# Inner matmul groups of two-level gate/up products wait for the token block they read

## The chip, the core and the metric

The kernel runs on one NeuronCore of a Trainium2 chip. The metric is device time in microseconds (us) for one execution. The engines are named as in the profile: PE is the tensor engine, PEld its weight loads, DVE the vector engine, ACT the scalar engine, POOL GpSimd and SP the engine that issues all DMAs here.

## What is computed

The input is one sequence of 2048 tokens of width 1024. Two kinds of layer alternate, A B A B, each with a residual and a layernorm ahead of it. Layer A is linear attention with 32 heads. Layer B is a bilinear gated block, and it is the one the change touches:

```
g = jnp.einsum("bsd,df->bsf", x, w_gate)      # d = 1024, f = 3584
u = jnp.einsum("bsd,df->bsf", x, w_up)
h = g * u
return jnp.einsum("bsf,fd->bsd", h, w_down)

x = x + _A_ref(_layernorm(x), A_wqkv, A_wo)
x = x + _B_ref(_layernorm(x), B_w_gate, B_w_up, B_w_down)
x = x + _A_ref(_layernorm(x), A_wqkv, A_wo)   # same weights again
x = x + _B_ref(_layernorm(x), B_w_gate, B_w_up, B_w_down)
```

## The kernel before

**Strassen products.** Layer B works on 1024 tokens at a time, so each of the two B layers has two passes (pass 0 and pass 1). Within a pass, a gate or up product of 256 feature columns by 1024 tokens is cut into 2 x 2 blocks and made from seven products instead of eight, named "1" to "7" (Strassen's method in Winograd's form). One such product is four matmuls of 512 columns, recorded at L1593. Some products, "1" and "5" in the first B layer and "1", "5", "3", "2" in the second, are cut a second time: seven inner products of two matmuls of 256 columns, recorded at L1663. The helper `l2_of` (L1634 on) sets these up. An inner group's left side is a block of weights or a sum of such blocks. Its right side is one of the four token blocks `b11`, `b12`, `b21`, `b22` of the operand, or one of three sums of them (`tp[0]` to `tp[2]`). Steps named `st1` (inner products 1 and 5), `st6`, `st7` and `direct` (inner products 2, 3, 4) issue them.

**One block is overwritten.** Inner product 7 needs `b22 - b12`, and the kernel writes that in place of `b12`. In the first pass of the first B layer, the first pair of gate/up units still uses "1" and "5" in their plain form and so needs `b12` unchanged. There the overwriting DVE operation is held back (the table `XD`) and is issued between the first pair and the second: for "1" after the elementwise product that the order table calls M5A, for "5" after M5B. The later passes overwrite `b12` ahead of time, among the layernorm work.

**What sets the order and the waits.** All work is put down by `P.add(engine, function, rd=..., wr=...)` in one fixed sequence; a string table `ORDERS` gives the sequence within a pair of units. Each engine runs its own list strictly in order. What an operation waits for comes from its ranges of bytes: `rd` and `wr` are looked up by pages of 32 bytes, and the operation depends on the last writer of every page it reads. `plan` then drops a wait that an earlier wait on the same engine already covers, and `emit` puts the first remaining wait on the operation's first instruction and each further wait ahead of it as an instruction of its own. A wait holds everything behind it on that engine.

Before the change, the four token blocks share one list of ranges `rx`, that of the whole operand, so an inner group that reads `b11` also depends on the last writer of `b12`.

The other names in the profile: L841 is the helper `tt` of all DVE additions, subtractions and multiplications in SBUF, L844 the helper `stt`, L1682 the DVE addition `join` that puts a sum of inner products into a PSUM bank, L1679 and L1689 the two ACT copies behind `st1`, L1598, L1607, L1773 and L1623 other ACT copies out of PSUM, L1499 the last product of layer A and L2104 and L2012 the down products.

Of the kernel before, what the change touches and what calls it, by code (L numbers as in the profile page):

```python
# [176 lines left out]
def _seg(base, n, stride, lo, hi):  # L177
    return [(base + i * stride + lo, base + i * stride + hi) for i in range(n)]


def build_kernel(nc, A_x, A_wqkv, A_wo, B_w_gate, B_w_up, B_w_down, out):
    _, S, D = A_x.shape
# [40 lines left out]
    def take(n, align=64):  # L223
        nonlocal off
        off = (off + align - 1) // align * align
        o = off
        off += n
        return o

    O_X = take(NST * D * 2)  # L230
    O_XT = take(KT * S * 2)
# [22 lines left out]
    O_T = RB  # L254
# [79 lines left out]
    with ExitStack() as es:  # L334
# [13 lines left out]
        def vh(o, n):  # L348
            return ah[:, o // 2: o // 2 + n]
# [72 lines left out]
        def R(o, n):  # L422
            return [(o, o + n)]
# [1133 lines left out]
        def layer_B(lnp, nxt, first):  # L1557
# [3 lines left out]
            def pair(ps_, p, l2):  # L1561
                s0 = ps_ * 1024
# [81 lines left out]
                def l2_of(q):  # L1644
# [9 lines left out]
                    wB, rB = units[1]["w"][q]  # L1654
                    x, rx = xb[q]
                    tp = [(vh(o, 512).rearrange("p (k s) -> p k s", s=256), R(o, 1024)) for o in (O_TP0 if jit else O_TP)[q]]
                    b11, b12, b21, b22 = [(x[:, 2 * k:2 * k + 2, 256 * c:256 * c + 256], rx) for k in range(2) for c in range(2)]
                    qs = {1: ((wA[:, 0:2, :], rA), b11), 2: ((wA[:, 2:4, :], rA), b21), 3: ((sp[3], rp[3]), b22), 4: ((wB[:, 2:4, :], rB), tp[2]),
                          5: ((sp[0], rp[0]), tp[0]), 6: ((sp[1], rp[1]), tp[1]), 7: ((sp[2], rp[2]), b12)}

# [68 lines left out]
                    return dict(st1=st1, st6=st6, st7=st7, st5=add5, direct=direct, s=s_of)  # L1729

                L = {q: l2_of(q) for q in l2}

                def fold_cp():
# [606 lines left out]
```

## Time and profile before

| | us |
|---|---|
| median of 3 runs | 1441.0 (1439.71 to 1441.69) |
| profiled execution | 1437.69 |
| its span, first to last instruction | 1436.0 |
| PE busy in it | 1423.3 (99%) |
| DVE busy | 1166.5 (81%) |
| ACT busy | 733.3 (51%) |
| mean DMA rate | 230 GB/s |

The granted clock of PE was 1.000 over the span. Times below are counted from the span's start. The first B layer's pass 0 begins about 238 us and its down products at 408 us; the second B layer's two passes begin about 955 us and 1192 us. A busy PE is the sum of pipelined matmul records, each of which lasts longer than the distance to the next one, so an idle time of PE as shown is a little shorter than the time by which the next matmul comes late.

### The profile page before, as it was taken

The numbers are of one execution on the slowest core, as the hardware profiler recorded it, in microseconds if no ns is written. First come the engines' busy times: TensorE is split into PE (matmuls) and PEld (weight loads), VectorE is DVE, ScalarE is ACT, GpSimd is POOL, SyncE is SP. The second block draws the span as 40 slices with busy tenths as digits, with TensorE's granted clock in tenths as the row PEclk, the third lists the DMA queues.
The fourth block names the chain that finished last, engine by engine and source line by source line (L and its number), as shares of the span: only waits on it lengthen the run. The fifth ranks groups of instructions, "written<-read, shape, count | busy, mean of one in ns | idle before, by whom it ended". The sixth has DMA issues, their size and how long they took to land.

```text
span 1436.0 us, 22438 instructions
## 1 busy us (share of the span) xinstructions
PE 1423.3 (99%) x8388; PEld 809.3 (56%) x8388; DVE 1166.5 (81%) x2012; ACT 733.3 (51%) x1538; POOL 314.2 (22%) x321
## 2 busy tenths in 40 slices
PE   9999999999999999999999999999999999999999
PEld 4444444555544455554764444456666477666658
DVE  7878887889879789878778878779877867777886
ACT  4752367677731155552256523567777115777521
POOL 4643632000013000003334346300000400000060
PEclk9999999999999999999999999999999999999999
DMA  6316868887878899995898067679985699778668
GB/s 234 107 26 189 178 137 199 244 292 243 298 262 286 283 320 315 274 271 177 261 362 207 34 188 154 151 216 270 280 271 198 227 284 324 256 258 265 211 185 258
DMA packets 393996, 330.15 MB, mean 230 GB/s; under 512 B 178336, under 2 KB 342048, under 8 KB 393376
## 3 DMA queue, kind: packets, MB, share of 16 engines
q1 hardware_dynamic: 393888, 328.72, 76.3%
q8 instruction: 66, 1.08, 0.3%
q14 instruction: 42, 0.34, 0.1%
HBM read 238.49 MB, written 66.58 MB: 212 GB/s over the span
## 4 chain that ended last, share of the span: by engine, by line
PE 95%; DVE 2%; ACT 1%; DMA 1%; issue 1%; SPq 0%; POOL 0%; DVEq 0%
PE ps L1593 27%; PE ps L1663 18%; PE ps L2104 14%; PE ps L2012 8%; PE ps L1401 8%; PE ps L1499 6%; PE ps L1167 6%; PE ps L971 5%; PE ps L981 3%; DVE arena L841 1%; PE ps L1413 1%; PE ps L1441 0%; DMA arena<-in_A_x_dram 0%; DVE arena L481 0%; SPq L441 0%
## 5 line engine op out<-in xcount | busy, mean ns | idle before, releaser
L841 DVE TENSOR_TENSOR arena<-arena 128x512 f16<-128x512 f16 (+9 forms) x780 | 480.6, 644 | 76.7 <-ACT arena L1707 45.1
L1593 PE MATMUL ps<-arena 128*128 128x512 f16 x1808 | 446.9, 379 | 0.6 <-ACT ps L1623 0.6
L1663 PE MATMUL ps<-arena 128*128 128x256 f16 x2324 | 312.2, 273 | 6.0 <-DVE arena L841 5.3
L844 DVE SCALAR_TENSOR_TENSOR arena<-ps,arena 128x512 f16<-128x512 f32 (+2 forms) x392 | 259.8, 684 | 38.8 <-PE ps L1593 16.3
L1663 PEld LDWEIGHTS ps<-arena 128*128 128x128 f16 (+1 forms) x2324 | 226.1, 98 | 109.8 <-DVE arena L841 6.3
L1593 PEld LDWEIGHTS ps<-arena 128*128 128x128 f16 (+1 forms) x1808 | 176.5, 98 | 141.7 <-ACT ps L1623 1.1
L2057 POOL TENSOR_TENSOR arena<-arena 128x512 f32<-128x512 f32 x56 | 87.3, 1564 | 596.5 <-ACT arena L2055 591.4
L2104 PE MATMUL ps<-arena 128*128 128x512 f16 (+1 forms) x952 | 206.9, 379 | 0.0
L1598 ACT ACTIVATE arena<-ps 128x512 f16<-128x512 f32 x224 | 133.9, 598 | 92.9 <-PE ps L1593 90.8
L2104 PEld LDWEIGHTS ps<-arena 128*128 128x128 f16 x952 | 93.1, 98 | 111.5
L1682 DVE TENSOR_TENSOR ps<-ps,arena 128x256 f32<-128x256 f32 x220 | 92.3, 428 | 39.5 <-PE ps L1663 23.0
L1679 ACT COPY ps<-ps 128x256 f32<-128x256 f32 x220 | 81.1, 369 | 84.3 <-PE ps L1663 78.0
L2012 PE MATMUL ps<-arena 128*128 128x256 f16 (+1 forms) x1078 | 119.1, 273 | 0.2
L1401 PE MATMUL ps<-arena 128*128 128x512 bf16 x512 | 115.4, 379 | 0.0
L2012 PEld LDWEIGHTS ps<-arena 128*128 128x128 f16 x1078 | 104.8, 98 | 14.2 <-DVE ps L2019 0.4
L1499 PE MATMUL ps<-arena 128*128 128x512 bf16 x512 | 111.5, 379 | 0.0
L2055 ACT ACTIVATE arena<-ps 128x512 f32<-128x512 f32 x48 | 28.7, 597 | 132.6 <-PE ps L2104 132.6
L1167 PE MATMUL ps<-arena 128*128 128x512 bf16 (+1 forms) x420 | 95.1, 379 | 0.4 <-DVE ps L1171 0.3
L1307 POOL TENSOR_TENSOR arena<-arena 128x1024 f16<-128x1024 f32 x32 | 80.0, 2501 | 69.1 <-DVE arena L1305 62.7
L1623 ACT COPY ps<-ps 128x512 f32<-128x512 f32 x112 | 64.2, 573 | 50.3 <-PE ps L1663 45.0
L1006 POOL TENSOR_TENSOR arena<-arena 128x512 f32<-128x512 f32 x60 | 73.5, 1244 | 69.4 <-DVE arena L1096 33.7
L1499 PEld LDWEIGHTS ps<-arena 128*128 128x128 f16 x512 | 50.1, 98 | 59.8
(80 smaller groups left out, 1261.6 us busy)
## 6 DMA issues: line engine op xcount, KB each, us to landing
arena<-w_scratch SPq DMA_DIRECT2D x84, 512.0 KB, 5.7
arena<-sp_scratch SPq DMA_DIRECT2D x56, 512.0 KB, 5.8
arena<-t_scratch SPq DMA_DIRECT2D x27, 896.0 KB, 5.6
arena<-in_B_w_down_dram SPq DMA_DIRECT2D x18, 896.0 KB, 6.7
w_scratch<-arena SPq DMA_DIRECT2D x28, 512.0 KB, 6.4
sp_scratch<-arena SPq DMA_DIRECT2D x28, 512.0 KB, 4.8
arena<-in_B_w_gate_dram SPq DMA_DIRECT2D x42, 256.0 KB, 5.3
arena<-in_B_w_up_dram SPq DMA_DIRECT2D x42, 256.0 KB, 3.2
```

The costliest lines, as they stand in the source:

```text
L841: P.add("dve", lambda e: e.tensor_tensor(out=out, in0=a, in1=b, op=op), rd=rd, wr=wr, prd=prd)
L844: P.add("dve", lambda e: e.scalar_tensor_tensor(out=out, in0=a, scalar=sc, in1=b, op0=ALU.mult, op1=op1), rd=rd, wr=wr, prd=prd)
L1167: P.add("pe", lambda e: [e.matmul(psb(bank), x[:, k, :], w[:, k, :], start=(start and k == 0), stop=(k == 3), skip_group_check=True) for k ...
L1401: return [e.matmul(psb(bank), xr[:, t, j * 128:(j + 1) * 128], pk[:, h, t, :], start=(t == 0), stop=(t == NST - 1)) for t in range(NST)]
L1499: return [e.matmul(psb(bank), xnT[:, g, i * 128:(i + 1) * 128], wp[:, g, dh * 512:(dh + 1) * 512], start=(dh == 0 and g == 0), stop=(g == ...
L1593: P.add("pe", lambda e: [e.matmul(psb(bank), w[:, k, :], x[:, k, :], start=(start and k == 0), stop=(k == 3), skip_group_check=True) for k ...
L1598: P.add("act", lambda e: e.activation(t, psb(bank), AF.Copy, scale=SG), prd=[bank], wr=r)
L1663: P.add("pe", lambda e: [e.matmul(psb(bank)[:, 256 * half:256 * half + 256], w[:, k, :], xx[:, k, :], start=(start and k == 0), stop=(k == ...
L1682: P.add("dve", lambda e: e.tensor_tensor(out=psb(dst[c])[:, 256:512], in0=lo, in1=c5, op=ALU.add), prd=[bk], rd=rc5, pwr=[dst[c]])
L2012: P.add("pe", lambda e: [e.matmul(psb(bank)[:, 256 * half:256 * half + 256], a[:, k, :], w[:, k, :], start=(start and k == 0), stop=(k == ...
L2057: P.add("pool", (lambda k2, x: lambda e: e.tensor_tensor(out=rtmp[k2], in0=rtmp[k], in1=x, op=ALU.add))(k2, x), rd=rx + rr(k), wr=rr(k2))
L2104: return [e.matmul(psb(bank), hv[:, 7 * hf + k, t * 128:(t + 1) * 128], w[:, k, :], start=(start and hf == 0 and k == 0), stop=(hf == 1 an ...
```

## The change

The whole-operand range is replaced by the range of the block that is read. For "5" in the form of the temporary T1 the rows are 1024 bytes apart, for "1", "2" and "3" they are rows of the transposed activations. No instruction is added, removed or moved on any engine; what waits for what is different. The lines behind it move down by five, so that L1663 becomes L1668.

```diff
-                    b11, b12, b21, b22 = [(x[:, 2 * k:2 * k + 2, 256 * c:256 * c + 256], rx) for k in range(2) for c in range(2)]
+                    if q == "5":
+                        base, st_ = O_T, 1024
+                    else:
+                        base, st_ = O_XT + 4 * (q != "1") * S * 2 + 2 * s0 + 1024 * (q == "3"), S * 2
+                    b11, b12, b21, b22 = [(x[:, 2 * k:2 * k + 2, 256 * c:256 * c + 256], _seg(base + 2 * k * st_, 2, st_, 512 * c, 512 * c + 512))
+                                          for k in range(2) for c in range(2)]
```

PE, first B layer, pass 0, the second pair: the last two plain products of the first pair, then `st1` of "1" (two groups of two matmuls, the first reading `b11`, the second `tp[0]`). The names in brackets are semaphores: s_dve, s_act count operations of those engines, names in d_ are DMAs (d_rr3 is a load of weights into ring slot 3). Before:

```order
L1593 MATMUL ps<-arena 128x512 [waits s_act]
L1593 MATMUL ps<-arena 128x512 x3
L1663 MATMUL ps<-arena 128x256 [waits s_dve]
L1663 MATMUL ps<-arena 128x256 x3
L1593 MATMUL ps<-arena 128x512 [waits s_act]
L1593 MATMUL ps<-arena 128x512 x3
```

After:

```order
L1593 MATMUL ps<-arena 128x512 [waits s_act]
L1593 MATMUL ps<-arena 128x512 x3
L1668 MATMUL ps<-arena 128x256 [waits d_rr3]
L1668 MATMUL ps<-arena 128x256
L1668 MATMUL ps<-arena 128x256 [waits s_dve]
L1668 MATMUL ps<-arena 128x256
```

The first group now waits for its weights alone, and the second for a DVE operation, which is no longer the overwriting of `b12` but the sum of weights that it reads.

PE, the same pair a little later: `st6` of "1", two plain products, then `st1` of "5" (again a group on `b11` and one on `tp[0]`), one plain product, and the groups behind it. Before:

```order
L1663 MATMUL ps<-arena 128x256 [waits s_act]
L1663 MATMUL ps<-arena 128x256
L1593 MATMUL ps<-arena 128x512 x8
L1663 MATMUL ps<-arena 128x256 [waits s_dve]
L1663 MATMUL ps<-arena 128x256 x3
L1593 MATMUL ps<-arena 128x512 x4
L1663 MATMUL ps<-arena 128x256 x4
```

After:

```order
L1668 MATMUL ps<-arena 128x256 [waits s_dve,s_act]
L1668 MATMUL ps<-arena 128x256
L1593 MATMUL ps<-arena 128x512 x8
L1668 MATMUL ps<-arena 128x256 [waits s_dve]
L1668 MATMUL ps<-arena 128x256
L1668 MATMUL ps<-arena 128x256 [waits s_dve]
L1668 MATMUL ps<-arena 128x256
L1593 MATMUL ps<-arena 128x512 [waits s_act]
L1593 MATMUL ps<-arena 128x512 x3
L1668 MATMUL ps<-arena 128x256 [waits s_dve]
L1668 MATMUL ps<-arena 128x256 x3
```

The one wait for DVE ahead of `st1`, which was for the overwriting of the "5" operand's `b12`, is now two waits for earlier DVE operations (the weights of "5" for this pair, and a sum of blocks of them), and three waits that it used to cover are stated: the sum of weights for `st6`, an ACT copy, and the `join` of "1".

ACT, the same pair: the copies behind the two `st1` and `st7`. Before:

```order
L1679 COPY ps<-ps 128x256 [waits s_pe]
L1689 COPY arena<-ps 128x256
L1623 COPY ps<-ps 128x512 [waits s_pe]
L1679 COPY ps<-ps 128x256 [waits s_pe]
L1598 ACTIVATE arena<-ps 128x512 [waits d_xs1,s_pe]
```

After:

```order
L1684 COPY ps<-ps 128x256 [waits s_act,s_pe]
L1694 COPY arena<-ps 128x256
L1623 COPY ps<-ps 128x512 [waits s_pe]
L1684 COPY ps<-ps 128x256 [waits s_dve,s_pe]
L1598 ACTIVATE arena<-ps 128x512 [waits d_xs1,s_pe]
```

Two ACT copies state a wait that PE's wait used to cover for them. In all, PE has nine waits more and ACT two; besides this pair they lie at the first groups of the second B layer's two passes. DVE, POOL and SP have the same lists and waits as before.

## The prediction

> **What bounds the kernel now.** I read the page's busy times first, then PE's waits, then the stretches by stage, then the timelines of PE, DVE and ACT around the one place where PE waits.
>
> ```profile
> PE 1423.3 (99%) x8388; PEld 809.3 (56%) x8388; DVE 1166.5 (81%) x2012; ACT 733.3 (51%) x1538; POOL 314.2 (22%) x321
> PE ps L1663 <- DVE arena L841: 5.3, 2, 3.3
> PE ps L1663 <- ACT arena L1707: 0.6, 2, 0.4
> 237.00:262.00 25.00, 19.10 (x100) 9.28 (x99) 15.17 (x36) 14.29 (x30) 2.98 (x6) 1.00 0.83 257
> 262.00:408.00 146.00, 146.00 (x844) 82.09 (x843) 125.66 (x288) 104.32 (x225) 0.74 (x2) 1.00 0.85 276
> 494.00:658.00 164.00, 164.00 (x949) 92.61 (x947) 137.18 (x303) 90.59 (x192) 6.98 (x16) 1.00 1.00 289
> ```
>
> PE is busy in 1423.3 of 1436.0 us: it is the bound, and only its 12.7 idle us can be won without doing less. The waits say (total, times, longest) that two stops of the inner groups for DVE make 5.3 us of these, the largest item. The stretches (columns: length, then busy PE, PEld, DVE, ACT and POOL, PE's clock, DMA share, GB/s) place them: 237 to 262 us has 19.10 of 25.00 busy, and the 146 us behind it are full. Time won at 247 to 255 us therefore reaches the end unless something behind makes PE stop again.
>
> ```profile
> 243.11 1.90 PE L1593 MATMUL ps<-arena 128*128 128x512 f16 x8 [0.58 <-ACT ps L1623]
> 246.99 0.61 PE L1663 MATMUL ps<-arena 128*128 128x256 f16 x4 [1.98 <-DVE arena L841]
> 247.44 1.89 PE L1593 MATMUL ps<-arena 128*128 128x512 f16 x8
> 249.17 0.38 PE L1663 MATMUL ps<-arena 128*128 128x256 f16 x2
> 249.38 1.89 PE L1593 MATMUL ps<-arena 128*128 128x512 f16 x8
> 254.59 0.61 PE L1663 MATMUL ps<-arena 128*128 128x256 f16 x4 [3.32 <-DVE arena L841]
> 259.37 0.82 PE L1663 MATMUL ps<-arena 128*128 128x256 f16 x6
> 245.59 1.35 DVE L841 TENSOR_TENSOR arena<-arena 128x256 f16<-128x256 f16 x5
> 249.59 0.43 DVE L1682 TENSOR_TENSOR ps<-ps,arena 128x256 f32<-128x256 f32 x1 [2.65 <-PE ps L1663]
> 249.93 2.61 DVE L841 TENSOR_TENSOR arena<-arena 128x1024 f16<-128x1024 bf16 x4
> 253.06 1.48 DVE L841 TENSOR_TENSOR arena<-arena 128x1024 f16<-128x1024 f16 x3
> 256.76 0.43 DVE L1682 TENSOR_TENSOR ps<-ps,arena 128x256 f32<-128x256 f32 x1 [2.22 <-PE ps L1663]
> 257.42 0.43 DVE L1682 TENSOR_TENSOR ps<-ps,arena 128x256 f32<-128x256 f32 x1 [0.23 <-ACT ps L1679]
> 259.82 2.48 DVE L841 TENSOR_TENSOR arena<-arena 128x1024 f16<-128x1024 f16 x4 [0.45 <-ACT arena L1773]
> 265.41 0.43 DVE L1682 TENSOR_TENSOR ps<-ps,arena 128x256 f32<-128x256 f32 x1 [0.65 <-PE ps L1663]
> 278.27 2.62 DVE L841 TENSOR_TENSOR arena<-arena 128x1024 f16<-128x1024 bf16 x4 [0.56 <-DMA arena<-in_B_w_down_dram]
> ```
>
> Each row is start, duration, instruction and the idle time ahead with what ended it. The two PE groups of four that stop are `st1` of "1" (246.99) and `st1` of "5" (254.59) of the second pair. What they wait for is the end of a DVE row: the five L841 end at 246.94, and the last of them overwrites `b12` for "1"; the three L841 end at 254.54, and the last of them overwrites `b12` for "5". Neither group reads `b12`.
>
> **The first wait.** Eight 512-column matmuls take 249.17 - 247.44 = 1.73 us from start to start. So the eight from 243.11 are done with the array at 244.84, and the next group comes 246.99 - 244.84 = 2.15 late (1.98 as idle, the rest is the pipelined end of the last record). By the new waits it needs its weights, loaded long before, and the first of the four weight sums that stood at the head of the L841 work ahead of 245. It starts at about 244.84. What is late next? `st6`, two groups on (4 x 0.11 + 1.73 us, so 247.02), waits for the two ACT copies behind `st1`:
>
> ```profile
> 245.16 0.60 ACT L1607 ACTIVATE arena<-ps 128x512 f16<-128x512 f32 x1
> 247.64 0.36 ACT L1679 COPY ps<-ps 128x256 f32<-128x256 f32 x1 [1.88 <-PE ps L1663]
> 247.91 0.38 ACT L1689 COPY arena<-ps 128x256 f32<-128x256 f32 x1
> ```
>
> ACT is free at 245.76, so the copies end by 246.5, half a microsecond before they are needed. The first wait goes whole: -2.15.
>
> **The second wait.** The eight matmuls from 249.38 end at 251.11, and `st1` of "5" comes at 254.59, 3.48 late (3.32 as idle). It now waits for the weights of "5" and a sum of them. That sum is in the row of 245.59 and done by 246.94; with the first 2.15 gone PE asks for it at 251.11 - 2.15 = 248.96. The second wait goes too: together -5.63.
>
> **Whether DVE stops PE later.** PE now runs 5.63 ahead of its old times and DVE must follow. Its `join` at 249.59 waited 2.65 for PE, so it moves by 2.15, to 247.44 (DVE is free at 246.94). The four L841 behind it read a block of w_down; they move from 249.93 to 247.78, and the load has this row (count, KB, us from issue to landing), with an issue at 240.51:
>
> ```profile
> 240.51 0.64 SPq L441 DMA_DIRECT2D arena<-in_B_w_down_dram  x1
> arena<-in_B_w_down_dram SPq DMA_DIRECT2D x1, 1024.0 KB, 7.2
> ```
>
> It lands at 247.7, about 0.1 ahead of the need. From there DVE has no idle time up to 254.54, so the overwriting for "5" ends at 252.4. The two joins at 256.76 and 257.42 had waited 2.22 for PE and 0.23 for ACT; they can now end at about 252.8 and 253.2. The PE group at 259.37, the first behind them that needs them, comes at 253.74. It does not stop, by half a microsecond. DVE has then given up 2.15 + 2.22 + 0.23 + 0.45 (259.82) = 5.05 of idle time, 0.58 less than PE's lead, and has another 0.65 at 265.41, where it waited for PE. So DVE catches up within a pair, with little over. At 278.27 it waits 0.56 for the next w_down load, whose issue stands on SP behind stores that wait for DVE's sums; if that load comes 5.05 and not 5.63 sooner, DVE is up to 0.58 later there, and a PE group soon behind it may stop for that much. Bounds for both waits together are thus -5.63 (all kept) and -5.05 (DVE's idle time alone). I take -5.3, between them.
>
> **The other places and the added waits.** At the first groups of the second B layer's passes nothing was lost to DVE:
>
> ```profile
> 955.56 1.47 PE L1663 MATMUL ps<-arena 128*128 128x256 f16 x12
> 957.47 1.48 PE L1663 MATMUL ps<-arena 128*128 128x256 f16 x12 [0.43 <-ACT arena L1707]
> 1197.65 1.48 PE L1663 MATMUL ps<-arena 128*128 128x256 f16 x12 [0.16 <-ACT arena L1707]
> 1203.09 0.60 PE L1663 MATMUL ps<-arena 128*128 128x256 f16 x4
> 965.73 2.35 PE L1663 MATMUL ps<-arena 128*128 128x256 f16 x20
> ```
>
> The stops of 0.43 and 0.16 are for ACT copies that the change leaves; 0. The added waits (nine on PE, two on ACT) are all for work that is done by then. Their price has no row of its own. But twenty matmuls at 0.11 from start to start (247.44 - 246.99 for four) make 2.25 us, and the twenty from 965.73 take 2.35: that leaves 0.10 for the end of the last and the six waits inside, at most 0.02 each. So I put the eleven at 0; the bound on the dear side is 0.2 in all, and nothing can be won by a wait. [...]
>
> **Sum.** Profiled: 1437.69 - 5.3 = 1432.4, with a span near 1430.7. The profiled execution lies 3.3 under the median 1441.0 (runs 1439.71 to 1441.69), so on the median the same difference gives 1435.7.
>
> **Rivals.**
> *Half of it.* DVE's late work takes the second wait's place: the load at 247.7 or the joins come a little later than reckoned, and PE stops at 253.74. To undo the whole second wait they would have to be 3.5 us late, with 0.5 in hand. Then only the first wait is won: 1441.0 - 2.15 = 1438.9, within measurement (0.2% is 2.9 us, about what a measurement can tell here from no change).
> *Nothing.* The gain is given back within the pass, where DMA engines are 0.85 busy. Against it: the pass at 494 to 658 runs PE full at a DMA share of 1.00. 1441.0.
> *Slower, by the w_down loads.* With the stops gone, transfers that had run in their shelter crowd the loads. Six w_down loads follow in this pass:
>
> ```profile
> arena<-in_B_w_down_dram SPq DMA_DIRECT2D x6, 1024.0 KB, 6.6
> DMA to landing us min/median/max: 6.0/7.1/9.1
> ```
>
> If each took the longest 9.1 in place of 6.6 and DVE and PE waited it out, 6 x 2.5 - 5.3 = +9.7, 1450.7. It decides from (5.3 + 2.9) / 6 = 1.4 us each. Against it: the loads are issued earlier as PE and DVE are, and the bytes are the same.
> *More, by the clock.* If the stops had let PE's clock fall, matmuls behind them would run slow, and removing the stops would win that too. Against it: granted clock 1.00 in 237 to 262, and four matmuls take 0.61 after each stop and 0.60 without one (1203.09). Half a clock for the length of the longer stop would be worth 1.7 us: 1434.0. [...]
>
> **Chances.** Both waits won 0.84 (1435.7); with the clock 0.02; half 0.07; nothing 0.04; slower 0.03. So faster by over 0.2% 0.86, within it 0.11, slower 0.03. The range for eight in ten: from 1434.0 (all 5.63 kept, runs 1 us apart from their median, or the clock) to 1438.5 (up to the half gain).
>
> **What would show it.** Right: PE's two waits for DVE L841 gone, `st1` at about 244.8 and 249.0, the join's 2.65 down to 0.5, PE idle 7.4 in all, and the later stages 5.3 sooner. A new PE wait for DVE L1682 between 253 and 285 would show DVE's lag, of 0.3 if I am right and of 3 in the half case. Wrong: PE stops for loads after 262, or DVE waiting longer for w_down.

## The result and the profile after

The changed kernel takes 1433.33 us (median of 5 runs, 1432.3 to 1433.82) against 1441.0 for the kernel before (5 runs, 1439.1 to 1441.69). The ratio is 0.9949, with a 95% interval of 0.9935 to 0.9964. So 7.7 us were won where 5.3 were forecast, and the time lies 0.7 us under the forecast's range. The two profiled executions, however, differ by what was forecast: 1437.69 and 1432.3, 5.4 apart, with spans of 1436.0 and 1430.6.

PE's waits of the changed kernel (total, times, longest), its longest items:

```profile
PE ps L448 <- POOL arena L444: 1.4, 1, 1.4
PE ps L1668 <- ACT arena L1712: 0.6, 2, 0.4
PE ps L1593 <- ACT ps L1623: 0.6, 1, 0.6
```

The item of 5.3 us for DVE L841 is gone. The place itself on PE and on DVE, from the timeline (start, duration, instruction, idle time ahead and what ended it), and the stretch of 237 to 262 us:

```profile
243.46 1.90 PE L1593 MATMUL ps<-arena 128*128 128x512 f16 x8 [0.58 <-ACT ps L1623]
245.19 0.60 PE L1668 MATMUL ps<-arena 128*128 128x256 f16 x4
249.30 0.60 PE L1668 MATMUL ps<-arena 128*128 128x256 f16 x4
254.07 0.82 PE L1668 MATMUL ps<-arena 128*128 128x256 f16 x6
247.78 0.43 DVE L1687 TENSOR_TENSOR ps<-ps,arena 128x256 f32<-128x256 f32 x1 [0.50 <-PE ps L1668]
252.64 0.76 DVE L1687 TENSOR_TENSOR ps<-ps,arena 128x256 f32<-128x256 f32 x2
273.10 2.62 DVE L841 TENSOR_TENSOR arena<-arena 128x1024 f16<-128x1024 bf16 x4 [0.69 <-DMA arena<-in_B_w_down_dram]
237.00:262.00 25.00, 24.39 (x132) 12.54 (x131) 18.39 (x44) 19.52 (x41) 3.12 (x7) 1.00 0.97 298
```

Both `st1` groups follow the work ahead of them without a stop, 5.6 us sooner than before once the 0.35 by which this execution was later at 243 is taken off (254.59 - 249.30 + 0.35). The `join` waits 0.50 for PE in place of 2.65. The group of six at 254.07 does not stop either. PE's idle time in all, 10.4 us, cannot be held against the 7.4 forecast, because 56 matmul records are missing from this trace. So the mechanism is as forecast, and the question is where another 2.4 us on the median come from.

### The profile page after: what moved, and what is told of

Its sections match the earlier page's. It is cut to its first block, busy times and chain, and to the rows that moved or that the text cites. A ratio compares the mean times of both kernels' runs of the same rounds, so it can differ in the third digit from the quotient of the medians.

```text
span 1430.6 us, 22386 instructions
## 1 busy us (share of the span) xinstructions
PE 1420.2 (99%) x8332; PEld 809.8 (57%) x8388; DVE 1167.1 (82%) x2012; ACT 733.5 (51%) x1538; POOL 314.6 (22%) x321
## 4 chain that ended last, share of the span: by engine, by line
PE 95%; DVE 2%; ACT 1%; issue 1%; POOL 1%; DMA 0%; SPq 0%; ACTq 0%
PE ps L1593 27%; PE ps L1668 18%; PE ps L2109 14%; PE ps L2017 8%; PE ps L1499 8%; PE ps L1401 8%; PE ps L1167 6%; PE ps L971 4%; PE ps L981 2%; PE ps L1413 1%; ACT arena L493 0%; DVE arena L841 0%; DMA arena<-in_A_x_dram 0%; PE ps L1441 0%; ACT arena L473 0%
## 5 line engine op out<-in xcount | busy, mean ns | idle before, releaser
L841 DVE TENSOR_TENSOR arena<-arena 128x512 f16<-128x512 f16 (+9 forms) x780 | 480.5, 644 | 76.4 <-ACT arena L1712 45.1
L1668 PE MATMUL ps<-arena 128*128 128x256 f16 x2324 | 312.1, 273 | 0.7 <-ACT arena L1712 0.6
L1668 PEld LDWEIGHTS ps<-arena 128*128 128x128 f16 (+1 forms) x2324 | 226.4, 98 | 104.0 <-DVE ps L1687 3.8
L1687 DVE TENSOR_TENSOR ps<-ps,arena 128x256 f32<-128x256 f32 x220 | 92.3, 428 | 34.5 <-PE ps L1668 18.3
```

What stands on the lines that cost most here:

```text
L841: P.add("dve", lambda e: e.tensor_tensor(out=out, in0=a, in1=b, op=op), rd=rd, wr=wr, prd=prd)
L1668: P.add("pe", lambda e: [e.matmul(psb(bank)[:, 256 * half:256 * half + 256], w[:, k, :], xx[:, k, :], start=(start and k == 0), stop=(k == ...
L1687: P.add("dve", lambda e: e.tensor_tensor(out=psb(dst[c])[:, 256:512], in0=lo, in1=c5, op=ALU.add), prd=[bk], rd=rc5, pwr=[dst[c]])
```

## The experiments

**The two kernels again.** The kernel before and the changed kernel were run once more without an edit, and the changed kernel a third time beside a later experiment.

> The kernel before once more, unchanged. It asks why the change won 7.7 us on the median where the two profiled executions differ by 5.4. Three theories. Clock: in the executions that take 1439 to 1442 us the stops at 247 and 251 us let PE's clock fall for a while (about 1.7 us each time), and the profiled one of 1437.7 escaped; then a run's mean clock reads 0.999 or 0.998 where its time is long. Landing: the x_scratch stores on which DVE's chain hangs land at other times from run to run, and the stops are longer by that; then the clock stays 1.000 and a profile of a long run shows a longer wait than 5.3 us in all. Profiling: long and short executions are a matter of the run alone and say nothing of the stops; then the waits read 5.3 in any profile. All expect a median of 1440 to 1441.5.

> The changed kernel once more, unchanged, for its runs' clocks. Clock theory: PE never stands for more than 0.6 us after the start, so every run has a mean clock of 1.000, the runs lie within 2 us of each other, and the median is 1433 to 1434; against the runs of before with clock 1.000 (1437.4 to 1438.1) it wins 4.5 to 5.3 us, against their median 6.5 to 7.5. If the clock were a matter of the run and not of the stops, runs of 0.999 and 0.998 appear here too.

> The changed kernel once more, beside the one with the earlier load: 1432.6 to 1433.5, every run at clock 1.000; its profile has a stop for DVE L1687 between 270 and 282 us of 0.3 to 0.9, with a DVE wait for w_down ahead of it.

The kernel before came to 1441.1 us again (ratio 1.0002, 0.9994 to 1.0011); one of its twelve runs took 4348.84 us, for a reason that is not known, and is left out of the table below. The profile was now of the longest of the other eleven, with a span of 1442.5 us. Its PE timeline, and the clock in stretches (length, busy PE, PEld, DVE, ACT and POOL, granted clock, DMA share, GB/s):

```profile
244.69 1.90 PE L1593 MATMUL ps<-arena 128*128 128x512 f16 x8 [0.58 <-ACT ps L1623]
248.56 0.61 PE L1663 MATMUL ps<-arena 128*128 128x256 f16 x4 [1.97 <-DVE arena L841]
249.01 2.90 PE L1593 MATMUL ps<-arena 128*128 128x512 f16 x8
257.38 1.04 PE L1663 MATMUL ps<-arena 128*128 128x256 f16 x4 [2.86 <-DVE arena L841]
259.92 1.91 PE L1663 MATMUL ps<-arena 128*128 128x256 f16 x8
246.40:249.70 3.30, 1.33 (x9) 0.74 (x9) 2.07 (x7) 1.43 (x4) 0.00 (x0) 1.00 1.02 339
249.80:253.10 3.30, 3.30 (x11) 1.32 (x9) 0.72 (x2) 1.74 (x4) 0.00 (x0) 0.50 1.15 295
253.20:256.50 3.30, 1.33 (x6) 0.39 (x4) 3.27 (x6) 0.60 (x1) 0.00 (x0) 1.00 1.08 377
256.60:263.30 6.70, 5.92 (x20) 3.00 (x21) 2.20 (x6) 1.57 (x4) 0.00 (x0) 0.50 0.27 77
263.40:270.00 6.60, 6.60 (x38) 3.59 (x37) 5.12 (x13) 4.55 (x10) 0.00 (x0) 1.00 0.02 6
```

The waits are no longer than in the first profile (1.97 and 2.86), so they did not grow with the time. Of the 6.5 us that this execution is longer, 1.6 lie ahead of the place (244.69 against 243.11). What differs at the place is the clock: it is 0.50 in the 3.3 us shown behind the first stop and again in 6.7 us that begin within the second, and eight matmuls that took 1.89 us now take 2.90. The median time rises as a run's mean clock falls to 0.998, and not further below that. The table takes the runs of all sessions in which each run's clock was listed, the repeat of the kernel before among its 76:

| mean clock of the run | kernel before: runs | median us | changed kernel: runs | median us |
|---|---|---|---|---|
| 1.000 | 7 | 1438.1 | 15 | 1432.7 |
| 0.999 | 44 | 1439.8 | 0 | |
| 0.998 | 12 | 1441.1 | 0 | |
| 0.995 to 0.997 | 13 | 1440.8 | 0 | |
| all | 76 | 1440.2 | 15 | 1432.7 |

Seven runs in 76 kept the full clock, and the first profile was such an execution. All 15 of the changed kernel kept it. At full clock the change wins 1438.1 - 1432.7 = 5.4 us; the other 2.1 is the clock. The ratios of the repeats are 0.9950 (0.9936 to 0.9963) and 0.9945 (0.9932 to 0.9957). Both expectations for the changed kernel were too high: 1432.64 where 1433 to 1434 were expected (and its runs lie 2.3 us apart, not within 2), and 1432.36 where 1432.6 to 1433.5 were. The stop for L1687 that the third was to show is not among PE's waits in its profile.

**Each product alone.** The narrowed ranges for one product of the first B layer's pass 0, the rest as before; for "5" the same with `q == "5"`.

```diff
-..., _seg(base + 2 * k * st_, 2, st_, 512 * c, 512 * c + 512))
+..., _seg(base + 2 * k * st_, 2, st_, 512 * c, 512 * c + 512) if jit and q == "1" else rx)
```

> The ranges are narrowed for product "1" of the first B layer's pass 0 alone; everything else as before. My step: the first wait is worth 2.15 us and the second stays, since the three L841 behind the join move 2.15 sooner and so does PE. Profile: no stop at the first st1, a stop of about 3.3 us at st1 of "5", span 1433.9, 2.1 under before. The rival that DVE is what counts: PE only waits longer at the second st1 (5.3), and nothing is won. If the extra gain of the median comes by the clock, the median is 1437 to 1439; if by the landing, the second stop keeps its spread.

> The ranges are narrowed for product "5" alone. My step: the first stop stays (2.0 idle), the second goes (3.48): span 1432.5 to 1433, some 3.2 to 3.5 under before, DVE's joins stopping PE for at most 0.3 behind it. The rival that the late work of DVE takes the place of the second wait: a new PE stop for DVE L1682 near 257 us and under 2 us won.

"1" alone: 1437.93 us, ratio 0.9981 (0.9972 to 0.9989). "5" alone: 1434.61, ratio 0.9961 (0.9949 to 0.9973). The profile of "1" alone shows the second stop with its full length and the clock that followed it; that of "5" alone the first stop, and what is behind it:

```profile
245.09 0.60 PE L1668 MATMUL ps<-arena 128*128 128x256 f16 x4
252.68 1.03 PE L1668 MATMUL ps<-arena 128*128 128x256 f16 x4 [3.32 <-DVE arena L841]
248.30:251.60 3.30, 1.06 (x5) 0.29 (x3) 3.27 (x6) 0.60 (x1) 0.00 (x0) 1.00 1.14 297
251.70:258.40 6.70, 5.72 (x20) 3.00 (x21) 2.17 (x6) 1.57 (x4) 0.00 (x0) 0.50 0.81 267
258.50:262.00 3.50, 3.50 (x21) 1.96 (x20) 2.20 (x8) 1.66 (x4) 0.00 (x0) 1.00 0.04 12
```

```profile
PE ps L1668 <- DVE arena L841: 2.0, 1, 2.0
PE ps L1593 <- ACT ps L1623: 0.6, 1, 0.6
PE ps L1668 <- DVE ps L1687: 0.5, 1, 0.5
```

Against the 1438.1 of the kernel before at full clock, "1" alone has 1436.0 there (two of its eleven runs) and "5" alone 1434.6 (all five): 2.1 and 3.5 us, near the two terms of the forecast (2.15 and 3.48). That they agree to a tenth is luck, since the seven runs behind the 1438.1 lie between 1437.4 and 1439.2. Neither wait comes back in the other's place. The spans of both profiles missed what was expected: 1436.6 for "1" (1433.9 expected), whose clock fell, and 1433.9 for "5" (1432.5 to 1433), where PE stopped for the joins for 0.5 and not for at most 0.3, and which was 0.9 later than the kernel before ahead of the place already.

**The stops filled.** The kernel before, with matmuls of no use put into the time in which PE stands; what they write is cleared by `st1`, so that they only add work. In three forms: both stops, the first alone (`q == "1"`), the second alone (`q == "5"`).

```diff
 def st1():
+    if jit and p == 1:
+        xw, rxw = xb["3"]
+        P.add("pe", lambda e: [e.matmul(psb(bk), ident, xw[:, 0, :], start=True, stop=True, ...)
+                               for _ in range(8 if q == "1" else 14)], rd=rxw + R(O_IDENT, 256), pwr=[bk])
     mm(1, bk, 0, True)
     mm(5, bk, 1, False)
```

> The kernel before, with 8 matmuls of 512 columns ahead of st1 of "1" and 14 ahead of st1 of "5" in the second pair, on data that is at hand, into the PSUM bank that st1 clears: they add work whose result is thrown away, and fill 1.73 of the 2.15 us and 3.02 of the 3.48 us in which PE stands. Clock theory: PE has no idle time left for its clock to fall, so the slow part of the spread goes and the median comes to 1437.5 to 1438.5. Landing theory: the waits end when they did, and the median stays at 1440 to 1441.5 with the same spread. If the filling reaches past the wait's end, up to 0.3 us is lost.

> The kernel before with the 8 matmuls ahead of st1 of "1" alone: the first stop is filled, the second (3.5 us) stands. Clock theory: if the second stop is what lets the clock fall, most runs still read 0.999 or less and the median stays within 0.5 us of the kernel before's (1440); the worst clocks, 0.997 and 0.996, where both stops told, go.

> The kernel before with the 14 matmuls ahead of st1 of "5" alone: the second stop is filled, the first (2.15 us) stands. Clock theory: product "5" narrowed alone left all five runs at 1.000, so the first stop seldom lowers the clock; most runs read 1.000 and the median is 1438 to 1439, as with both filled (1438.6). If the first stop told as much as the second, the median lies halfway to 1440.2.

With both filled, PE does 22 matmuls more and the kernel is faster: 1438.62 us, ratio 0.9990 (0.9981 to 0.9998), nine of eleven runs at 1.000. Its waits still end when DVE ends:

```profile
247.56 0.61 PE L1663 MATMUL ps<-arena 128*128 128x256 f16 x4 [0.25 <-DVE arena L841]
251.68 3.19 PE L1688 MATMUL ps<-arena 128*128 128x512 f16 x14
255.16 0.61 PE L1663 MATMUL ps<-arena 128*128 128x256 f16 x4 [0.30 <-DVE arena L841]
```

So PE's idle time, not the length of the waits, is what lowered the clock. With the first filled alone the median is 1440.32 (ratio 1.0003, 0.9994 to 1.0012) and eight of eleven runs read under 1.000: the second stop is enough by itself. With the second filled alone it is 1439.18 (ratio 0.9994, 0.9985 to 1.0003), and here the expectation missed: the first stop was to lower the clock seldom, and six of eleven runs read 0.999, though the same stop had left all five runs of "5" alone at 1.000. Five runs are few, and the difference may be chance. These eleven are the cleanest price of a fall: five at 1.000 have a median of 1437.86, six at 0.999 one of 1439.67, 1.8 us apart. The profile of one of the six:

```profile
243.56 1.90 PE L1593 MATMUL ps<-arena 128*128 128x512 f16 x8 [0.58 <-ACT ps L1623]
247.42 0.61 PE L1663 MATMUL ps<-arena 128*128 128x256 f16 x4 [1.96 <-DVE arena L841]
247.86 2.82 PE L1593 MATMUL ps<-arena 128*128 128x512 f16 x8
245.30:248.60 3.30, 1.34 (x9) 0.79 (x9) 2.02 (x7) 1.44 (x4) 0.00 (x0) 1.00 1.02 361
248.70:252.00 3.30, 3.30 (x10) 1.32 (x9) 0.85 (x2) 1.69 (x4) 0.00 (x0) 0.50 1.18 288
252.10:255.00 2.90, 2.90 (x15) 1.33 (x14) 2.87 (x6) 0.60 (x1) 0.00 (x0) 1.00 1.08 374
```

**DVE made late.** The changed kernel, with one small product on DVE repeated.

```diff
-tt(hx, mb[:, 0:512], mb[:, 512:1024], ALU.mult, rb, hr)
+for _ in range(5 if p == 0 and dst == "2" else 1):
+    tt(hx, mb[:, 0:512], mb[:, 512:1024], ALU.mult, rb, hr)
```

> The changed kernel, with the last product of the first pair's M5B on DVE done five times in place of once (four times 0.4 us that change nothing in the result), so that the overwriting for "5" and the two joins behind it come about 1.7 us later. My step: st1 of "5" does not wait for any of this and stays at 249.3; the joins had about 0.9 us in hand before the PE group of six at 254.07, so PE stops there for 0.8 to 1.0 us, and a little more is lost because DVE has less idle time than before to catch up: span 1 to 1.5 us over the changed kernel's. The rival that DVE's work is off PE's path by more than I reckoned: no new stop and the same time.

1434.45 us (four runs), 1.8 over the changed kernel's 1432.64 in the same session, where 1 to 1.5 were expected of the span. `st1` of "5" does not wait, the group of six stops as reckoned, and a second stop follows a round later:

```profile
250.16 0.60 PE L1668 MATMUL ps<-arena 128*128 128x256 f16 x4
256.10 0.83 PE L1668 MATMUL ps<-arena 128*128 128x256 f16 x6 [1.02 <-DVE ps L1687]
281.26 0.83 PE L1668 MATMUL ps<-arena 128*128 128x256 f16 x6 [1.44 <-DVE ps L1687]
```

The first stop of 1.02 fits how little the joins were reckoned to have in hand. The second, which the expectation had too small, is at the place that the next experiment is about; 0.90 of such a stop stands in the profile of the changed kernel of the same session too.

**The w_down load sooner.** On SP, in the same pass, the load goes ahead of the stores.

```diff
-if j:
-    wd_store(j - 1)
 if j < NJ // 2:
     wd_load(j)
+if j:
+    wd_store(j - 1)
```

> The changed kernel with one swap on SP in the first B layer's pass 0: each w_down load is issued ahead of the four t_scratch stores of the block before, not behind them. In the two profiles of the changed kernel the load near 265 us came late by 0.7 and 1.6 us for DVE, and PE stopped for DVE's joins near 278 us by 0.3 and 0.9. If that load is what is left of the second wait, it now lands 2 to 3 us sooner, DVE waits for none, PE has no stop for L1687 in the pass, and the median falls by 0.3 to 0.9 against the changed kernel. If the stop is DVE's own lag, the stop stays and the time is the same.

1431.98 us against 1432.36 of the changed kernel in the same session; ratio to the kernel before 0.9943 (0.9930 to 0.9955). Four of its five runs lie between 1431.93 and 1432.03 at a clock of 1.000; the fifth, 1432.42, reads 0.999; it is only 0.4 us longer, and where its clock fell is not known. (The profiled one, 1431.93, reads 1.000.) The median is the lowest of all versions, but the runs of the two kernels overlap (1431.82 to 1432.7 unswapped), so 0.4 us is not clear of noise. The late load is seen in the repeat of the changed kernel (first two lines) and in that of the kernel before (the other two), and is not in the waits of the swapped one (second fence, its DVE waits for loads of w_down from 237 to 300 us):

```profile
273.81 2.62 DVE L841 TENSOR_TENSOR arena<-arena 128x1024 f16<-128x1024 bf16 x4 [1.59 <-DMA arena<-in_B_w_down_dram]
278.50 0.83 PE L1668 MATMUL ps<-arena 128*128 128x256 f16 x6 [0.90 <-DVE ps L1687]
284.63 2.62 DVE L841 TENSOR_TENSOR arena<-arena 128x1024 f16<-128x1024 bf16 x4 [1.20 <-DMA arena<-in_B_w_down_dram]
289.31 0.83 PE L1663 MATMUL ps<-arena 128*128 128x256 f16 x6 [0.50 <-DVE ps L1682]
```

```profile
DVE arena L841 <- DMA arena<-in_B_w_down_dram: 0.2, 1, 0.2
```

So the changed kernel can lose time at 278 us, 0.9 in that execution. But the kernel before loses 0.50 there in its second profile, behind a load that is 1.20 late, and the other two profiles of the changed kernel have no such stop among PE's waits. That the change makes this load later is not shown.

**The other places.** The narrowed ranges everywhere but in the first B layer's pass 0 (`if not jit else rx`).

> The ranges are narrowed in every pass but the first B layer's pass 0, where they stay whole. My step: at the first groups of the second B layer nothing was lost, and the added waits cost nothing, so the two stops of 2.0 and 3.3 us stay and the time is that of the kernel before within 0.5 us (1439.5 to 1440.5). If the other places held a hidden gain, it shows here.

1439.70 us, ratio 0.9999 (0.9990 to 1.0008): no gain and no cost that can be told, with the two stops as before. The interval reaches from -1.4 to +1.2 us, so it bounds the added waits only roughly. Closer is the profile of the changed kernel: the eight matmuls ahead of `st1` take 245.19 - 243.46 = 1.73 us from start to start and the four of `st1` 0.44 (the next group starts at 245.63), the pace of before, with the new waits among them. Of the eleven waits, by the instructions in the two traces, four are instructions of their own, two on PE and two on ACT, so the change does add four such instructions.

## Why the prediction was right in its cause and wrong in its size

**The first wait, -2.15, and the second, -3.48:** right. Alone they gave about 2.1 and 3.5 us at full clock, together 5.4 (5.3 forecast), and PE came to `st1` of "5" 5.6 us sooner.

**DVE's lag, 0.3 of the 5.63:** right in the place, not shown in size. The w_down load was late for DVE by 0.69, 1.59 and 0.74 in the three profiles of the changed kernel, and PE stopped behind it for 0.9 in one of them. In the two profiles of the kernel before it was late by 0.56 and 1.20, so the lateness varies without the change too.

**The other places and the added waits at 0:** nothing speaks against it. The run in which only the other places were changed shows no cost, but could not have shown one under about 1.2 us. In the changed kernel's profile the four matmuls of `st1` of "1" take 0.44 us with the new waits among them, where they took 0.45 before.

**The failed step** is in the sum: the profiled execution lies 3.3 under the median, "so on the median the same difference gives 1435.7". That took the distance between the profile and the median for an offset that both kernels share. Most of it, about 2.1 of the 3.3, was the cost of the stops themselves in the executions in which the clock fell, and it belonged to what the change removes. The changed kernel's profile lies only 1.0 under its median. The term that was mis-sized is therefore the clock's, in the rival "More, by the clock": it was put at a chance of 0.02 because the one profiled execution showed a clock of 1.00 and 0.61 us behind each stop. The runs showed that execution to be one of few: 69 of 76 runs of the kernel before read under 1.000. The price given there, 1.7 us, took half a clock for the length of the longer stop, which the first profile does not show; the later ones showed 0.50 for 3.3 us behind the first stop and for 6.7 behind the second. It was near what was measured (1.8 for one fall, 2.1 on the median), and its time of 1434.0 is 0.7 from the result. The forecast named the mechanism and dismissed it on a sample of one. The range's low end had room for the clock alone, without any scatter. With the measured sizes, the sum is -5.4 - 2.1 = -7.5; the first comparison gave -7.7 and the repeats -7.1 (1432.64 against 1439.77) and -8.0 (1432.36 against 1440.36).

**The rivals:** "Half of it" and "Nothing" did not happen. "Slower, by the w_down loads" needed 1.4 us from each of six loads; one load was late, its stop cost PE 0.9 at most, and it is not shown that the change makes it later.

## What to carry to other kernels

A profile is one execution: where its time lies at the edge of the runs, ask what the other executions pay, and read the clock of every run before an offset is carried over. Here a stop of PE cost its length and, in some runs, slow matmuls behind it (eight took 2.90 us in place of 1.89), so two stops of 2.15 and 3.48 us were worth more than one profile shows (7.5 us on the median, and 5.4 at full clock). A range noted for a whole operand, where a block is read, can put a wait on an operation that nobody needs yet; look for it where an in-place update stands between.

## What was not expected of the hardware

The clock fell after stops shorter than the time that it then stayed at half speed. In the run with the second stop filled, PE's eight matmuls ended at 245.29 (243.56 + 1.73) and the next started at 247.42: 2.13 us without work, and from 248.7 to 252.0 the clock read 0.50. In the first profile, 3.48 us without work left it at 1.00. Nor was PE idle throughout ahead of the fall: the stretch of 245.30 to 248.60 had PE busy for 1.34 of 3.30 us by its records.

The half clock lasted one length or about twice that. The stretches shown with the experiments read 0.50, and 1.00 from 0.1 us ahead of them and behind them: 3.3 to 3.5 us behind the first stop, in the repeat of the kernel before and in the run with the second stop filled, and 6.7 to 6.9 us behind the second, in that repeat and in the run of "1" alone. Between its two falls the repeat reads 1.00 for 3.3 to 3.5 us. In the two profiles of the first comparison the clock record has one stretch at full clock each, from 6.86 to 1437.05 us and from 7.33 to 1430.69. Their lengths, 1430.18 and 1423.36, differ by 6.83, twice 3.413, and are 419 and 417 times 3.413. An estimate from these lengths is that in these five executions the clock changed only at edges 3.413 us apart, which lay differently against the program's start in each. Laid out from 6.86, such edges lie at 249.21, 252.62 and 256.03 in the first profile and cut its second stop of 3.48 us into 1.51 and 1.97 us. Two stretches of that profile, about these two periods:

```profile
249.20:252.60 3.40, 2.08 (x11) 0.84 (x9) 2.98 (x6) 1.48 (x3) 0.00 (x0) 1.00 1.20 281
252.60:256.00 3.40, 1.41 (x9) 0.90 (x10) 1.90 (x4) 0.65 (x2) 0.00 (x0) 1.00 0.69 281
```

By this estimate the same stop cost or not by where an edge fell in it: 1.97 us without work between two edges left the clock at 1.00, and the 2.13 above were followed by 0.50. With a limit between these two and an edge anywhere, the first stop alone would lower the clock in 0.38 to 0.48 of the runs (6 of 16 read under 1.000) and the second alone in 0.77 to 0.87 (17 of 22 did). For both together it would leave 0.13 to 0.23 of the runs at full clock, where 7 of 76 were, so the account is not complete. No run was made to find the limit or to test the edges.
